# A decode step of attention plus a gated MLP on one core: loads of four heads instead of two, K transposed as 32-bit words, and the rest of the kernel fitted to that

## The chip, the core and the metric

The kernel runs on one core of one Trainium2 chip. The time is the device time of one execution in microseconds (us); the kernel before took 699.09 us (median of 3 runs, 698.64 to 700.31). A core has five engines with a queue of instructions each: TensorE (PE in the profile; its loading of the stationary operand is listed apart as PEld), VectorE (DVE), ScalarE (ACT), GpSimd (POOL) and SyncE (SP). Here SP issues nearly all DMAs. Engines wait for one another and for DMAs through semaphores only, and each takes its instructions in order.

## The reference

One token for each of 4 sequences. Attention reads a cache of 4,096 keys and values for each of 4 x 32 heads, 128 numbers each, in bf16: 128 MiB of K and 128 MiB of V. The second branch is a small gated MLP ("gMLP") on the same input.

```python
x = A_x                                  # 4 x 1 x 640
xn = layernorm(x)
q = (xn @ wq)  -> (4, 32 heads, 1, 128)
scores = q . k_cache * 128 ** -0.5       # k_cache 4 x 32 x 4096 x 128
p = softmax(scores)
o = p . v_cache                          # v_cache 4 x 32 x 4096 x 128
attention = o.reshape(4, 1, 4096) @ wo   # wo 4096 x 640
z = gelu(xn @ w_in)                      # w_in 640 x 1728
z1, z2 = z[..., :864], layernorm(z[..., 864:])
gmlp = (z1 * (w_sp * z2 + b_sp)) @ w_out # w_out 864 x 640
out = x + attention + gmlp
```

## The kernel before

**Units.** A unit is one 2 MB load of K or of V: two heads of one sequence, 128 partitions with 64 keys each, so that a partition's row is 16 KB (`load_unit`, L248, on SP's queue). There are 64 units of K and 64 of V. Eight units (four heads, four sequences) make a group; softmax is done once for each of the 8 groups, and V of a group runs `VDU` = 10 units behind its K. K has a pool of four 2 MB tiles, V another of four.

**K.** Scores need the head dimension on the partitions, so TensorE transposes K: a 128x128 block of bf16 is loaded as stationary operand, and the identity is streamed through it (L273, 64 blocks a unit, 8 to a PSUM tile `pst`, of which there are three). DVE and ACT take turns to copy the `pst` tiles to SBUF (`evacuate`, L262 and L264; tile `kT`). Then come the scores (`emit_S`, L293): the query, placed in a row of zeros (`qz_all`) so that each unit writes rows of its own, against `kT`, 512 columns at a time, four column groups side by side.

**Softmax** (`chain_stage`): a maximum over S, turned by TensorE (L308, a transpose of 128x1 fp32) and spread again by TensorE (L319), the exponential on ACT (L326), P transposed by TensorE (L337, 16 matmuls a group), and copied into `Zb`, in which zeros surround it, by DVE and ACT.

**V** (`emit_V`, L365): stationary is a 32-column window of `Zb`, moving is V, 512 columns at a time. After four units the result is copied (`emit_O`, L374, L375), its diagonal blocks are picked by fp32 matmuls (`emit_sel`, L383), divided by the row sums (L387) and multiplied with `wo` into `proj` (L396). At the end `proj` is cast (L447) and stored (L448, L449). The last unit of V comes in two loads.

**Start.** x and wq are loaded (L87, L94), the input is normalised, q is computed (L155). The weights of the gMLP are loaded at unit 2 into three tiles of V's pool (L174, L178), which wq still holds; the branch is computed at units 5 and 6 (L191, L201, L230), w_in being read with a stride of 9 columns.

**Order.** The program is written as one loop over half units, with a table `sched` of what is called at which half unit. SP takes its loads in that order, and a load whose tile isn't free holds up all behind it.

Of the kernel before, what the change touches and what calls it, by code (L numbers as in the profile page):

```python
# [8 lines left out]
ACT = mybir.ActivationFunctionType  # L9
# [7 lines left out]
def kernel(  # L17
# [13 lines left out]
):  # L31
    nc = tc.nc
# [3 lines left out]
    assert Sq == 1 and Dh == P and D % P == 0 and B == 4  # L36
    DC = D // P
    HP = 2
    M = P // HP
    T = Sk // M  # L40
    NP = 8
    TP = T // NP
    assert TP == 8
    HG = 4
    G = HG * B
    NG = H // HG
    NHP = HG // HP
    UPG = NHP * B
    NU = NG * UPG
    BLK = T // 4  # L50
    F2 = B_w_in.shape[1]
    Fh = F2 // 2
    FP = 96
    FC = Fh // FP
    assert FP * FC == Fh
# [5 lines left out]
    VDU = UPG + 2  # L61
# [6 lines left out]
    ppool = ctx.enter_context(tc.tile_pool(name="ppool", bufs=2))  # L68
    opool = ctx.enter_context(tc.tile_pool(name="opool", bufs=2))
    wopool = ctx.enter_context(tc.tile_pool(name="wopool", bufs=2))  # L70
# [11 lines left out]


# [5 lines left out]
    wq_v = A_wq.rearrange("(c p) n -> p c n", p=P)  # L89
    wq_t = []  # L90
    for i, (c0, c1) in enumerate(((0, 2), (2, 4), (4, 5))):
        wt = vpool.tile([P, 2, H * Dh], BF16, tag="v", name=f"wq{i}")
        for c in range(c0, c1):
            nc.sync.dma_start(out=wt[:, c - c0, :], in_=wq_v[:, c, :])  # L94
            wq_t.append(wt[:, c - c0, :])
# [10 lines left out]
    QS = 32  # L106
    qz_all = const.tile([P, (H * B + 1) * QS], BF16)
    nc.gpsimd.memset(qz_all[:], 0.0)
    ZB = T * 8 + 8
    Zb = []  # L110
    for i in range(2):
        zt = const.tile([P, NHP, B * ZB], BF16, name=f"Zb{i}")
        nc.gpsimd.memset(zt[:], 0.0)
        Zb.append(zt)
# [4 lines left out]
    I16 = const.tile([P, G], F32)  # L119
    nc.vector.tensor_tensor(out=I16[:], in0=I32[:, 0:16], in1=I32[:, 16:32], op=ALU.add)  # L120


    xf = const.tile([B, D], F32)
    nc.vector.tensor_copy(out=xf[:], in_=x_bf[:])  # L124
    ssum = small.tile([B, 1], F32, tag="ln_s")
    nc.vector.reduce_sum(out=ssum[:], in_=xf[:], axis=AX.X)
# [13 lines left out]
    for c in range(DC):  # L140
        nc.tensor.transpose(xT_ps[:, c, :], xn_bf[:, c * P:(c + 1) * P], ident_bf[:B, :B])  # L141
# [338 lines left out]
```

## Time and profile before

| | |
|---|---|
| median of 3 runs | 699.09 us (698.64 to 700.31) |
| the profiled execution | 698.35 us |
| its span, first to last instruction | 696.6 us |
| read from HBM | 282.24 MB, 405 GB/s over the span |
| busy: PE, PEld, DVE, ACT, POOL | 75%, 56%, 32%, 40%, 2% |
| loads of 2 MB from issue to landing, median | K 34.2 us, V 35.1 us |
| transposes of K (L273) | 4096, the wait before them mostly for the load of K |
| copies of `pst` to `kT` | 256 on ACT, 256 on DVE |

Read it as follows. The share of busy time says little by itself, since PE's spans overlap. The rows "GB/s" and "DMA" cut the span into 40 slices of 17.4 us: they show where the loads ran and where they didn't. The view of windows gives the same numbers for any stretch, with the TensorE clock that was granted in it (1.00 is full speed). The timeline gives single instructions, or runs of like ones, with start and duration.

### The profile page before, as it was taken

The numbers are of one execution on the slowest core, as the hardware profiler recorded it, in microseconds if no ns is written. First come the engines' busy times: TensorE is split into PE (matmuls) and PEld (weight loads), VectorE is DVE, ScalarE is ACT, GpSimd is POOL, SyncE is SP. The second block draws the span as 40 slices with busy tenths as digits, with TensorE's granted clock in tenths as the row PEclk, the third lists the DMA queues.
The fourth block names the chain that finished last, engine by engine and source line by source line (L and its number), as shares of the span: only waits on it lengthen the run. The fifth ranks groups of instructions, "written<-read, shape, count | busy, mean of one in ns | idle before, by whom it ended". The sixth has DMA issues, their size and how long they took to land.

```text
span 696.6 us, 15065 instructions
## 1 busy us (share of the span) xinstructions
PE 523.3 (75%) x6781; PEld 391.6 (56%) x6781; DVE 225.9 (32%) x384; ACT 278.3 (40%) x311; POOL 12.7 (2%) x13
## 2 busy tenths in 40 slices
PE   0998999877777776777778687778768787886644
PEld 0886777655655554556466466556556665664322
DVE  8312454333222432333323332224223332332100
ACT  0433676444343443444444354345334344443000
POOL 7000000000000000000000000000000000000000
PEclk9976999999899999998989998899988999899555
DMA  8996999999999999999999999999999999999992
GB/s 338 403 357 254 360 428 425 427 426 419 425 426 427 423 422 425 426 428 422 424 426 426 428 419 428 426 427 421 423 423 431 423 425 422 430 424 423 413 424 115
DMA packets 24456, 283.22 MB, mean 407 GB/s; under 512 B 2396, under 2 KB 6504, under 8 KB 7144
## 3 DMA queue, kind: packets, MB, share of 16 engines
q1 hardware_dynamic: 24320, 282.26, 96.9%
q8 instruction: 53, 0.87, 0.5%
q14 instruction: 11, 0.09, 0.0%
q0 software_dynamic: 64, 0.00, 0.0%
q10 hardware_dynamic: 8, 0.00, 0.0%
HBM read 282.24 MB, written 0.01 MB: 405 GB/s over the span
## 4 chain that ended last, share of the span: by engine, by line
DMA 77%; PE 18%; ACT 3%; issue 1%; DVE 1%; SPq 0%; ACTq 0%; DVEq 0%
DMA v<-in_A_v_cache_dram 42%; DMA k<-in_A_k_cache_dram 34%; PE pst L273 10%; ACT kT L262 3%; PE S L293 3%; PE misc L191 2%; PE O L365 2%; PE proj L230 0%; SPq L94 0%; PE misc L383 0%; DVE Zb L264 0%; PE ptp L337 0%; ACT Zb L262 0%; PE proj L396 0%; PE misc L201 0%
## 5 line engine op out<-in xcount | busy, mean ns | idle before, releaser
L262 ACT COPY kT<-pst 128x1024 bf16<-128x1024 bf16 x256 | 254.4, 1012 | 305.0 <-PE pst L273 304.6
L273 PE MATMUL pst<-ident_bf,k 128*128 128x128 bf16 x4096 | 300.8, 239 | 95.9 <-DMA k<-in_A_k_cache_dram 90.8
L273 PEld LDWEIGHTS <-k 128*128 128x128 bf16 x4096 | 275.4, 109 | 141.0 <-DMA k<-in_A_k_cache_dram 111.1
L264 DVE COPY kT<-pst 128x1024 bf16<-128x1024 bf16 x256 | 177.1, 692 | 330.7 <-PE pst L273 330.5
L293 PE MATMUL S<-kT,qz_all 128*32 128x512 bf16 x1024 | 110.7, 385 | 8.1 <-ACT kT L262 8.1
L365 PE MATMUL O<-v,Zb 128*32 128x512 bf16 x1024 | 80.0, 418 | 19.1 <-DMA v<-in_A_v_cache_dram 19.1
L365 PEld LDWEIGHTS <-Zb 128*32 128x32 bf16 x1024 | 31.8, 101 | 52.0 <-issue 28.8
L293 PEld LDWEIGHTS <-qz_all 128*32 128x32 bf16 x1024 | 32.7, 95 | 37.8 <-issue 17.8
L383 PEld LDWEIGHTS misc<-I,O_sb 128*128 128x128 f32 x128 | 18.5, 216 | 13.9 <-ACT O_sb L374 12.5
L374 ACT COPY O_sb<-O 128x256 f32<-128x256 f32 x16 | 6.0, 373 | 45.9 <-PE O L365 45.8
L375 DVE COPY O_sb<-O 128x256 f32<-128x256 f32 x16 | 6.8, 424 | 51.6 <-ACT O_sb L374 50.9
L383 PE MATMUL misc<-I,O_sb 128*128 128x8 f32 x128 | 20.5, 280 | 3.3 <-ACT O_sb L374 2.9
L191 PEld LDWEIGHTS <-w_in 128*96 128x96 bf16 x90 | 15.6, 267 | 0.8 <-DMA w_in<-in_B_w_in_dram 0.4
L191 PE MATMUL misc<-xnT,w_in 128*96 128x4 bf16 x90 | 15.8, 312 | 0.0
L326 ACT ACTIVATE p_bf<-S,negmax 128x512 bf16<-128x512 f32 x8 | 5.5, 687 | 21.6 <-DVE negmax L322 21.6
L141 PE MATMUL misc<-ident_bf,xn_bf 4*128 4x4 bf16 x5 | 0.3, 165 | 14.6 <-DVE xn_bf L138 14.6
L264 DVE COPY Zb<-ptp 64x256 bf16<-64x256 bf16 x16 | 6.7, 417 | 13.7 <-PE ptp L337 10.6
L396 PE MATMUL proj<-wo,oT 128*4 128x320 bf16 x64 | 7.8, 326 | 4.1 <-DVE oT L387 4.1
L124 DVE CAST xf<-x_bf 4x640 f32<-4x640 bf16 x1 | 10.3, 10287 | 1.2 <-DMA x_bf<-in_A_x_dram 1.2
L337 PE MATMUL ptp<-ident_bf,p_bf 128*64 128x128 bf16 x128 | 9.6, 225 | 1.1 <-ACT p_bf L326 1.1
L348 PE MATMUL misc<-ds,ones_f 128*128 128x16 f32 x16 | 4.0, 329 | 8.0 <-DVE ds L329 8.0
L337 PEld LDWEIGHTS <-p_bf 128*64 128x64 bf16 x128 | 7.3, 111 | 4.5 <-issue 2.8
(70 smaller groups left out, 79.8 us busy)
## 6 DMA issues: line engine op xcount, KB each, us to landing
k<-in_A_k_cache_dram SPq DMA_DIRECT2D x64, 2048.0 KB, 34.2
v<-in_A_v_cache_dram SPq DMA_DIRECT2D x63, 2048.0 KB, 35.1
wq<-in_A_wq_dram SPq DMA_DIRECT2D x5, 1024.0 KB, 11.1
wo<-in_A_wo_dram SPq DMA_DIRECT2D x8, 640.0 KB, 36.0
v<-in_A_v_cache_dram SPq DMA_DIRECT2D x2, 1024.0 KB, 17.3
w_in<-in_B_w_in_dram SPq DMA_DIRECT2D x1, 1296.0 KB, 31.1
w_out<-in_B_w_out_dram SPq DMA_DIRECT2D x1, 1080.0 KB
w_in<-in_B_w_in_dram SPq DMA_DIRECT2D x1, 864.0 KB
```

The costliest lines, as they stand in the source:

```text
L124: nc.vector.tensor_copy(out=xf[:], in_=x_bf[:])
L191: nc.tensor.matmul(zT_ps[:FP, part * FC + fc, :], lhsT=w[:, fc, :], rhs=xnT[:, c, :], start=(c == 0), stop=(c == DC - 1))
L262: nc.scalar.copy(out=dst, in_=src)
L264: nc.vector.tensor_copy(out=dst, in_=src)
L273: nc.tensor.transpose(pst[:, e, :], k_sb[:, pc * TP + e, :], ident_bf[:])
L293: nc.tensor.matmul(S_ps[32 * q:32 * q + 32, :, :], lhsT=qz_all[:, w0:w0 + 32], rhs=kT[:, :, hd, :], start=(ul == 0 and bt == 0 and hd == 0 ...
L337: nc.tensor.transpose(ptp[hd * M:(hd + 1) * M, e, :], p_bf[:, e, :], ident_bf[:])
L365: nc.tensor.matmul(O_ps[32 * q:32 * q + 32, :, :], lhsT=Z[:, hp, w0:w0 + 32], rhs=vv[:, half, e, :, :], start=(b == 0 and half == 0 and e ...
L374: nc.scalar.copy(out=O_sb[:, 0:2, :], in_=O_ps[:, 0:2, :])
L375: nc.vector.tensor_copy(out=O_sb[:, 2:4, :], in_=O_ps[:, 2:4, :])
L383: nc.tensor.matmul(oh[:], lhsT=O_sb[:, j, :], rhs=sel[:, j, :, :], start=(j == 0), stop=(j == 3))
L396: nc.tensor.matmul(proj[32 * hf:32 * hf + B, 0:NO2], lhsT=oT[:, hd, :], rhs=wo_t[:, hp * HP + hd, hf * NO2:(hf + 1) * NO2], start=False, s ...
```

## The change

- **Loads.** A unit is now four heads of one sequence: 4 MB, 128 keys on a partition, rows of 32 KB (L278). There are 32 units of K, 32 of V, four to a group. K, V, wq and the gMLP's weights share one pool of five 4 MB tiles. wq comes in two loads with rows of 24 and 16 KB; its rows are dealt to partitions in another order, and so are xn's columns.
- **K as words.** The K tile is read as fp32: one word is two neighbouring bf16 numbers of a key. A 128x128 block of words is transposed with the fp32 identity (L303); 64 blocks a unit of twice the size, four to a `pst` tile of 2 KB a partition. `pst` is copied as 1024 bf16 as before (L292, L294). In `kT` the even and the odd numbers of a key alternate, and a partition holds one word. So the query is permuted by a matmul (L182), and the scores take two matmuls that read every second number of `kT` (L321). Two zero-padded tiles `QZ` are filled for each group by POOL (L191).
- **P.** The maximum goes through 32x32 transposes on DVE (L329, L336) instead of TensorE, and P is turned by one DVE transpose of 128x512 (L349). POOL copies it into `Zb`, four copies for each pair of sequences (L362).
- **V.** As before (L386), with a whole 512-column matmul over four keys' rows. The last unit differs: V itself is stationary, 128 blocks of 128x128, and four columns of P are streamed (L479). It comes in loads of 64, 32, 16 and 16 keys. The result needs neither the copy nor the picking.
- **gMLP.** Its weights are loaded behind unit 7 of K, and it runs in the middle of the stream. w_in is loaded as rows of 17,280 bytes and read without stride.

What SP issues at the start, before (the names are the tiles with their numbers; L94 is wq, L174 and L178 are the gMLP's weights):

```order
L94 DMA wq_96<-in_A_wq_dram 128x4096 x2
L94 DMA wq_99<-in_A_wq_dram 128x4096 x2
L94 DMA wq_102<-in_A_wq_dram 128x4096
L248 DMA k_325<-in_A_k_cache_dram 128x8192
L248 DMA k_424<-in_A_k_cache_dram 128x8192
L248 DMA k_530<-in_A_k_cache_dram 128x8192
L174 DMA w_in_576<-in_B_w_in_dram 128x3x1728
L174 DMA w_in_578<-in_B_w_in_dram 128x2x1728
L178 DMA w_out<-in_B_w_out_dram 96x5760
L248 DMA k_644<-in_A_k_cache_dram 128x8192
L248 DMA k_750<-in_A_k_cache_dram 128x8192
```

And now, from wq to the second load of V:

```order
L97 DMA wq_93<-in_A_wq_dram 128x12288
L97 DMA wq_95<-in_A_wq_dram 128x8192
L278 DMA k_335<-in_A_k_cache_dram 128x16384
L278 DMA k_464<-in_A_k_cache_dram 128x16384
L278 DMA k_598<-in_A_k_cache_dram 128x16384
L278 DMA k_732<-in_A_k_cache_dram 128x16384
L278 DMA k_868<-in_A_k_cache_dram 128x16384
L278 DMA v_959<-in_A_v_cache_dram 128x16384
L278 DMA k_1049<-in_A_k_cache_dram 128x16384
L278 DMA v_1137<-in_A_v_cache_dram 128x16384
```

No load of gMLP weights stands between the first loads of K any more. Further on in the same queue, around the eighth and ninth unit of K, they stand now:

```order
L278 DMA v_1309<-in_A_v_cache_dram 128x16384
L278 DMA k_1400<-in_A_k_cache_dram 128x16384
L208 DMA w_gmlp<-in_B_w_in_dram 128x8640
L211 DMA w_gmlp<-in_B_w_out_dram 128x6x640
L212 DMA w_gmlp<-in_B_w_out_dram 96x640
L278 DMA v_1490<-in_A_v_cache_dram 128x16384
L278 DMA k_1574<-in_A_k_cache_dram 128x16384
```

They take one of the five tiles, between a load of K and one of V.

The last instructions of PE before, from the last matmul with V on:

```order
L365 LDWEIGHTS Zb_122
L365 MATMUL O<-v_8972,Zb_122 32x512
L383 MATMUL misc_8994<-I_124,O_sb 128x8 x4
L396 LDWEIGHTS oT
L396 MATMUL proj<-wo_8764,oT 4x320
```

And now: picking (L465) and eight matmuls for the three earlier sequences, then 128 pairs for the last unit of V, then eight matmuls (the pairs and the projections are shown once each):

```order
L465 MATMUL misc_6281<-I_136,O_sb 128x8 x4
L411 LDWEIGHTS oT
L411 MATMUL proj<-wo_6197,oT 4x320
...
L479 LDWEIGHTS v_6274
L479 MATMUL ol<-Zb_154,v_6274 128x4
...
L411 LDWEIGHTS oL
L411 MATMUL proj<-wo_6197,oL 4x320
```

Picking has moved ahead of the last unit's matmuls; behind them stand one DVE multiplication (L480) and the eight matmuls of the projection.

The core of the diff:

```diff
-    HP = 2
-    M = P // HP
+    HG = 4
+    M = P // HG
     T = Sk // M
-    kpool = ctx.enter_context(tc.tile_pool(name="kpool", bufs=4))
-    vpool = ctx.enter_context(tc.tile_pool(name="vpool", bufs=4))
-    ktpool = ctx.enter_context(tc.tile_pool(name="ktpool", bufs=10))
+    kvpool = ctx.enter_context(tc.tile_pool(name="kvpool", bufs=5))
+    ktpool = ctx.enter_context(tc.tile_pool(name="ktpool", bufs=2))
...
+    def load_gmlp_weights():
+        wt = kv_tile("w_gmlp")
+        n_in = DC * F2
+        w_in = wt[:, 0:n_in].rearrange("p (c f) -> p c f", c=DC)
+        nc.sync.dma_start(out=w_in, in_=B_w_in.rearrange("(p c) f -> p c f", c=DC))
+        w_out = wt[:, n_in:n_in + FC * NOUT].rearrange("p (c n) -> p c n", c=FC)
+        nf = (FC - 1) * P
+        nc.sync.dma_start(out=w_out[:, 0:FC - 1, :], in_=B_w_out[0:nf, :].rearrange("(c p) n -> p c n", p=P))
+        nc.sync.dma_start(out=w_out[:FL, FC - 1, :], in_=B_w_out[nf:Fh, :])
...
+    def load_unit(cache, key, u, cuts=(0, T)):
+        g, b = divmod(u, B)
+        t_sb = kv_tile(f"{key}{u}")
+        src = cache[b, g * HG:(g + 1) * HG].rearrange("e (m t) d -> (e m) (t d)", t=T)
+        for t0, t1 in zip(cuts[:-1], cuts[1:]):
+            nc.sync.dma_start(out=t_sb[:, t0 * Dh:t1 * Dh], in_=src[:, t0 * Dh:t1 * Dh])
...
+    def emit_T(u, ch):
+        kw = state[("k", u)][:].bitcast(F32)
+        kT = ktpool.tile([P, KP, HG, M, 2], BF16, tag="kT", name="kT")
+        for pc in range(4):
+            pst = ps_t.tile([P, 4, P], F32, tag="pst", name="pst")
+            for e in range(4):
+                k = ch * KP + pc * 4 + e
+                nc.tensor.transpose(pst[:, e, :], kw[:, k * P:(k + 1) * P], ident_f[:])
+            evacuate(kT[:, pc * 4:(pc + 1) * 4].rearrange("p e h m w -> p (e h m w)"),
+                     pst[:].rearrange("p e m -> p (e m)").bitcast(BF16))
...
+        for w in range(2):
+            for hd in range(HG):
+                w0 = 16 + (hd * B + b) * 32 - (b * NCH + ch)
+                nc.tensor.matmul(S_ps[32 * hd:32 * hd + 32, :, :], lhsT=qz[:, w, w0:w0 + 32],
+                                 rhs=kT[:, :, hd, :, w], start=(b == 0 and ch == 0 and w == 0),
+                                 stop=(b == B - 1 and ch == NCH - 1 and w == 1))
...
+        nc.vector.transpose(x[:].rearrange("p e b c -> p (e b c)"), p_bf[:].rearrange("p k m -> p (k m)"))
...
+    def z_fill(g, bb):
+        x = state[("x", g)]
+        for hd in range(HG):
+            r0 = 32 * hd
+            dst = Zb[bb][r0:r0 + 32, :].rearrange("p (b y) -> p b y", y=ZL)[:, :, 0:1024].rearrange(
+                "p b (e c) -> p e b c", c=32)[:, :, :, hd * 4:hd * 4 + 4]
+            nc.gpsimd.tensor_copy(out=dst, in_=x[r0:r0 + 32, :, 2 * bb:2 * bb + 2, :])
...
-    at(2 * 2, load_gmlp_weights)
-    at(2 * 5, gmlp_branch)
-    at(2 * 6, gmlp_out)
+    at(NCH * 7, load_gmlp_weights)
+    at(NCH * 8 + 2, gmlp_branch)
+    at(NCH * 8 + 3, gmlp_out)
...
+    TAIL = (0, 64, 96, 112, 128)
...
+            for t in range(T):
+                c, e = divmod(t, 32)
+                zc = Zb[1][:, ZL + e * 32:ZL + e * 32 + 16].rearrange("p (h c) -> p h c", c=NCH)[:, :, c]
+                nc.tensor.matmul(ol_ps[:], lhsT=vv[:, t, :], rhs=zc, start=(t == 0), stop=(t == T - 1))
+            nc.vector.tensor_tensor(out=oL[:, :, 3:4], in0=ol_ps[:, :, None], in1=rinv[:, :, 3:4], op=ALU.mult)
+            emit_proj(g, oL, last=True)
```

More of the change, by code (lines that the diff above doesn't have):

```diff
@@ L81, in misc_ps, with kv_tile @@
         return ps_m.tile(shape, dtype, tag="misc", name=f"misc{misc_ctr[0]}")
+    KV = T * Dh
+    def kv_tile(name):
+        return kvpool.tile([P, KV], BF16, tag="kv", name=name)
     x_flat = A_x.rearrange("b s d -> (b s) d")
@@ L353, in emit_V @@
-    def emit_V(v, half):
-        g, hp, b, h = unit_info(v)
-        if b == 0 and half == 0:
+        kT = state.pop(("kT", u, ch))
+        qz = QZ[g % 2]
+        for w in range(2):
+            for hd in range(HG):
[3 more added lines that the diff above has]
+                                 stop=(b == B - 1 and ch == NCH - 1 and w == 1))
```

456 lines of the change are left out of this document (216 added, 240 removed).

## The prediction

> **What bounds the kernel now.** I read the page's slices first, then the chain that ended last, then the windows.
>
> ```profile
> PEclk9976999999899999998989998899988999899555
> DMA  8996999999999999999999999999999999999992
> GB/s 338 403 357 254 360 428 425 427 426 419 425 426 427 423 422 425 426 428 422 424 426 426 428 419 428 426 427 421 423 423 431 423 425 422 430 424 423 413 424 115
> DMA v<-in_A_v_cache_dram 42%; DMA k<-in_A_k_cache_dram 34%; PE pst L273 10%; ACT kT L262 3%; PE S L293 3%; PE misc L191 2%; PE O L365 2%; PE proj L230 0%; SPq L94 0%; PE misc L383 0%; DVE Zb L264 0%; PE ptp L337 0%; ACT Zb L262 0%; PE proj L396 0%; PE misc L201 0%
> ```
>
> From the sixth slice to the last but one the loads run at 413 to 431 GB/s with all DMA engines busy, and three quarters of the chain are loads of K and V. This is a kernel bound by its loads, except in the first five slices and the last. What the change can win lies there; what it can lose is the rate in between. The windows price the two ends:
>
> ```profile
> 15.00:20.00 5.00, 2.52 (x89) 2.53 (x90) 2.42 (x10) 0.29 (x1) 0.00 (x0) 1.00 0.79 320
> 30.00:52.00 22.00, 21.60 (x223) 18.66 (x220) 5.54 (x8) 9.16 (x9) 0.00 (x0) 0.82 1.01 363
> 52.00:60.00 8.00, 5.42 (x30) 5.16 (x30) 1.60 (x10) 1.81 (x3) 0.00 (x0) 0.50 1.02 430
> 60.00:68.00 8.00, 7.62 (x91) 5.60 (x92) 2.99 (x6) 2.95 (x4) 0.00 (x0) 0.72 0.27 113
> 68.00:90.00 22.00, 20.40 (x295) 15.22 (x288) 9.76 (x15) 14.14 (x15) 0.00 (x0) 1.00 0.95 354
> 100.00:640.00 540.00, 416.35 (x5543) 314.88 (x5544) 176.89 (x298) 234.03 (x261) 0.00 (x0) 0.91 1.01 425
> 676.00:690.00 14.00, 6.12 (x52) 1.72 (x47) 0.00 (x0) 0.00 (x0) 0.00 (x0) 0.50 0.57 238
> ```
>
> The last three columns are granted clock, DMA share and GB/s. Against 425, 60 to 68 us loses 8 x (1 - 113/425) = 5.9 us, 68 to 90 loses 22 x (1 - 354/425) = 3.7, 30 to 52 loses 3.2 though the engines were busy there (short rows), 15 to 20 loses 1.2. The timelines of SP and PE name the cause of the big hole:
>
> ```profile
> 6.19 16.32 SPq L174 DMA_DIRECT2D w_in<-in_B_w_in_dram  x2
> 22.62 0.40 SPq L178 DMA_DIRECT2D w_out<-in_B_w_out_dram  x1
> 23.07 57.02 SPq L248 DMA_DIRECT2D k<-in_A_k_cache_dram  x7
> ...
> 17.77 4.41 PE L155 MATMUL misc<-xnT,wq 128*128 128x4 bf16 x160 [0.26 <-DVE xnT L143]
> ...
> 41.62 15.12 PE L191 MATMUL misc<-xnT,w_in 128*96 128x4 bf16 x87
> ...
> 60.38 2.56 PE L230 MATMUL proj<-w_out,uT 96*4 96x320 bf16 x18 [2.25 <-DVE uT L223]
> ```
>
> w_in waits for wq's tiles until q is done, with K loads behind it. Then PE spends 41.6 to 62.9 us on the gMLP, transposes nothing, and K's four tiles stay full.
>
> **The change part by part.** The sum starts from the profiled execution's own 698.35 us (span 696.6 and 1.75 around it), 0.74 below the median of the runs.
>
> *Start and gMLP.* Ahead of the first wait SP now issues wq and three units of K, 17.8 MB; at 425 GB/s they last until about 45 us. The fourth K waits for wq's tile, so for q, done at 22.2 us; if PE is two units late, that still hides. The gMLP's weights follow unit 7 of K; their tile is the next but four to be used again, so 39 us of loads (four of 4.19 MB / 425 GB/s = 9.87 us) cover its use. Its 70 matmuls read without stride; at q's 4.41 us / 160 they take 2 us, and even at L191's pace 12; chain and second part add some 5. While PE waits in them, V and the next K are in flight. So 5.9 + 3.7 go. Of the 3.2 I take 2.5: w_in gets long rows, w_out does not (bounds 0 and 3.2). The 1.2 stay: POOL's two tiny loads of w_sp and b_sp are issued behind its memsets as before. Together **12.1 us**.
>
> *K on PE.* This is the price the trace doesn't show: an fp32 transpose of 128x128 in a row of such. The nearest rows:
>
> ```profile
> L308 PE MATMUL misc<-ident_f,m x8: 270/270/272, 95.2 to 641.8; 128*1 128x128 f32 x8
> ...
> L273 PE MATMUL pst<-ident_bf,k x4096: 216/219/314, 22.7 to 639.0; 128*128 128x128 bf16 x196
> ...
> 128.89 1.07 PE L273 MATMUL pst<-ident_bf,k 128*128 128x128 bf16 x16
> 129.88 0.62 PE L293 MATMUL S<-kT,qz_all 128*32 128x512 bf16 x8
> 130.33 1.04 PE L365 MATMUL O<-v,Zb 128*32 128x512 bf16 x16
> ...
> 131.85 1.07 PE L383 MATMUL misc<-I,O_sb 128*128 128x8 f32 x8
> ...
> 690.61 1.88 PE L383 MATMUL misc<-I,O_sb 128*128 128x8 f32 x8 [0.47 <-ACT O_sb L374]
> ```
>
> A single fp32 transpose with 128 streamed columns takes 270 ns against 219 for bf16: streaming costs some 50 ns more, about 105 in a row where bf16 takes (1.07 - 0.22) / 15 = 0.057. Loading 128 fp32 columns as stationary is shown by L383: (1.07 - 0.26) / 7 = 0.116 us a pair at full clock, (1.88 - 0.38) / 7 = 0.214 at half clock. If loading and streaming overlap, as in the bf16 rows, a transpose takes **0.116**; bounds are 0.057 and, one after the other at half clock, about 0.42. I take 0.116, the nearest row. Then a unit of K needs 64 x 0.116 = 7.4 us, where 64 blocks of half the bytes took 3.7. The scores keep their number of matmuls for each byte: 32 in eight rounds of four, (0.62 - 0.38) = 0.24 a round at most, 1.9 us; V the same, (1.04 - 0.38) / 3 = 0.22 a round, 1.8. PE needs 11.1 us for a unit of K and one of V, whose loads take 19.7. While only K is loaded (four and a half units), it needs 9.3 of 9.9. Copies from `pst` are as many and as large for each byte: eight on ACT at 1.012 us and eight on DVE at 0.692 a unit, inside the 9.9:
>
> ```profile
> L262 ACT COPY kT<-pst 128x1024 bf16<-128x1024 bf16 x256 | 254.4, 1012 | 305.0 <-PE pst L273 304.6
> ...
> L264 DVE COPY kT<-pst 128x1024 bf16<-128x1024 bf16 x256 | 177.1, 692 | 330.7 <-PE pst L273 330.5
> ```
>
> So this part costs **nothing on the path**, and its cover is 8 us in 19.7. Reading every second number of `kT` is not shown; doubled scores would be 1.9 more, still covered. If PE fell behind in the K phase, five tiles hold 39 us of loads; even 16 us a unit would stall the loads by 3 to 5 us only.
>
> *Softmax.* Removed: 16 transposes of P and two small PE steps a group; added: three DVE transposes and eight POOL copies of 256 numbers a partition. The large DVE transpose lies between nothing and the 0.692 of a copy of 1024; a POOL copy I put under 1 us. On PE a whole unit of K (9 us) stands between the last scores and the first use of `Zb`, and covers them. POOL has nothing else to do. A single `wo` tile makes SP wait for the last projection, with K behind it; that projection comes right behind the last V of its group, with two loads (19 us) still in flight.
>
> *Rate.* Rows of 8 KB (wq) and of 16 KB moved:
>
> ```profile
> 4.00:15.00 11.00, 0.00 (x0) 0.00 (x0) 10.83 (x6) 0.00 (x0) 9.29 (x5) 1.00 1.01 425
> 110.00:150.00 40.00, 35.03 (x505) 25.79 (x508) 14.69 (x23) 20.74 (x23) 0.00 (x0) 0.96 1.01 426
> ```
>
> One more doubling may bring half of that 0.2% again, **0.8 us** (bounds 3 us either way). Instructions are fetched by DMA too:
>
> ```profile
> q8 instruction: 53, 0.87, 0.5%
> ```
>
> From 676 to 690 us only 57% of the DMA engines still work: some end about 14 x 0.43 = 6 us behind the others. If fetching makes them late, 4590 matmuls in the program instead of 6700 take 31% of it away, **1.9 us** (bounds 0 and 1.9).
>
> *The end.* From the landing of the last V:
>
> ```profile
> 689.09 1.05 PE L365 MATMUL O<-v,Zb 128*32 128x512 bf16 x8 [1.43 <-DMA v<-in_A_v_cache_dram]
> ...
> 690.59 0.42 DVE L375 COPY O_sb<-O 128x256 f32<-128x256 f32 x1 [16.68 <-ACT O_sb L374]
> ...
> 692.74 0.70 PE L396 MATMUL proj<-wo,oT 128*4 128x320 bf16 x4 [0.26 <-DVE oT L387]
> 693.48 0.48 DVE L447 CAST o_bf<-proj 64x320 bf16<-64x320 f32 x1 [0.80 <-PE proj L396]
> ```
>
> Before: 693.48 - 689.09 = 4.4 us to the cast, 3.1 behind it. Now the last 16 pairs take 0.44 (q's 28 ns each), draining and the multiplication 0.5, eight projections instead of four 0.70 + 0.5: 2.2 us. The rest stays. **2.2 us** go (bounds 1.5 and 2.5).
>
> Sum: 698.35 - 12.1 - 0.8 - 1.9 - 2.2 = 681.35, forecast **681.3 us**, 2.4% less.
>
> **The rivals.**
>
> *PE at half clock becomes the bound (slower).* Half clock is granted where PE mostly loads weights: 52 to 60 us, in L191, at 0.50. An fp32 transpose spends more on loading than on streaming. At half clock a pair of units takes 64 x 0.214 = 13.7 plus 16 rounds of scores and V at 0.42 (eight matmuls of L365 in 1.05 us above, two rounds at clock 0.5) = 6.7 plus 0.3 for the rest, 20.7 us against 19.7 for its loads: 1.0 x 27.5 pairs = 27 us, **708 us**. It turns slower once a pair passes 19.7 + 17 / 27.5 = 20.3 us, so only if the clock stays low almost throughout; at full clock a transpose would have to take (20.3 - 4.0) / 64 = 0.25 us. Against it: 68 to 90 us, full of transposes, had clock 1.00, and a PE that is the bound is never idle. The Trainium skill ("TensorE: Matmul & The Clock Gate", Part 4: PE-mode transpose) says that transposes do not count as PE being busy, so the full clock does not engage; by that rule this rival would be the forecast. The row of 68 to 90 us speaks against the rule.
>
> *Loading and streaming do not overlap.* Then a transpose takes 0.116 + 0.105 = 0.22 us, a pair 18.1 at full clock: covered, but the K phase needs 16 us a unit, and any low clock shows. 3 to 12 us more: **684 to 693 us**. Nothing in the trace shows two fp32 transposes in a row, so nothing decides.
>
> *The hole only moves.* Five tiles for K, V and gMLP together may be held longer than I think around unit 8, or in the K phase. Half of the 9.6 us idle comes back: **686 us**. For it: SP takes loads strictly in order. Against: the reckoning of 39 us.
>
> **How the numbers follow.** Forecast (loads bound throughout) 0.73; the hole moves 0.06; no overlap 0.09; half clock or a price above 0.25 us 0.10; a loss of rate with the long rows that ends within 0.3% of before or above, 0.02. The forecast's own range: 681.3 with the 0.7 of w_out and 3 of the rate below and 6 us of uneven ending gone gives 673; with 3 of the rate, 2.5 and 1.9 unearned 689. The middle rivals reach to 693, so the range is 673 to 693. A difference under 0.3% (2.1 us) can't be told from none. Faster 0.87, same 0.02, slower 0.11.
>
> **What would show it.** Right: 420 GB/s or more in every slice from the second to the last but one, no hole around 60 us nor at the gMLP's new place; L303 in runs at about 0.12 us each; PE waiting for loads of K in the middle; some 5.3 us from the last landing to the end. Wrong: SP waiting for transposes while the DMA share is under 0.9; L303 at 0.2 us or more; clock 0.5 through the middle; slices below 410 GB/s with the engines busy, which would put it on the 32 KB rows.

## The result and the profile after

The changed kernel takes **677.74 us** (median of four runs, 677.69 to 678.79) against 698.87 (697.99 to 700.31) for the kernel before in the same session: ratio 0.970, 95% interval 0.968 to 0.972. The profiled execution took 678.79 us with a span of 676.9.

The page of the kernel after, its slices, the queue of instruction fetches and the shares of the chain that ended last:

```profile
PEclk9999998788878989688898878987787998967865
DMA  8999999999999999999999999999999999999994
GB/s 324 431 429 429 433 423 429 407 430 432 416 429 431 431 433 417 429 434 431 429 419 433 427 431 428 422 433 432 429 417 431 431 429 433 423 425 432 409 417 171
...
q8 instruction: 36, 0.59, 0.4%
...
DMA 58%; PE 32%; ACT 6%; DVE 3%; issue 1%; SPq 0%; ACTq 0%; DVEq 0%
```

No slice from the second to the last but one is below 407 GB/s, and the hole of before (357, 254 and 360 GB/s in the third to the fifth slice) is gone. The prediction had asked for 420 or more in each; seven lie between 407 and 419. PE's share of the chain has grown from 18% to 32% while DMA is still busy throughout: PE is later than before, but the loads do not wait for it.

Windows price it. Three that follow each other and cover the span before, then five after; the last three columns are the granted clock, the share of the DMA engines and GB/s:

```profile
0.00:90.00 90.00, 67.45 (x877) 55.88 (x878) 38.62 (x61) 33.68 (x36) 12.72 (x13) 0.89 0.89 346
90.00:660.00 570.00, 437.72 (x5776) 327.73 (x5777) 185.59 (x318) 243.92 (x274) 0.00 (x0) 0.90 1.01 425
660.00:696.60 36.60, 18.09 (x136) 8.00 (x128) 1.66 (x5) 0.74 (x2) 0.00 (x0) 0.50 0.65 275
```

```profile
0.00:90.00 90.00, 61.72 (x659) 45.45 (x663) 39.10 (x81) 43.78 (x45) 8.27 (x26) 1.00 0.97 410
90.00:120.00 30.00, 26.56 (x256) 19.10 (x244) 11.51 (x18) 15.90 (x16) 0.00 (x0) 0.94 1.01 425
120.00:160.00 40.00, 27.67 (x287) 19.54 (x281) 10.67 (x30) 15.25 (x19) 3.79 (x10) 0.79 1.01 417
160.00:640.00 480.00, 363.99 (x3214) 259.81 (x3212) 155.37 (x265) 199.45 (x211) 20.73 (x55) 0.86 1.01 429
640.00:676.90 36.90, 21.56 (x264) 12.10 (x264) 1.72 (x6) 0.58 (x1) 0.74 (x2) 0.55 0.71 293
```

A stretch of t us at r GB/s loses t x (1 - r/425) against the old steady rate. That gives a ledger of the two profiled executions, which lie 698.35 - 678.79 = 19.6 us apart:

| | before, us lost | after | gain | predicted |
|---|---|---|---|---|
| start (0 to 90 us) | 16.7 | 3.2 | 13.5 | |
| gMLP at its new place (120 to 160) | | 0.8 | -0.8 | |
| start and gMLP together | | | **12.7** | 12.1 |
| rate in the middle (160 to 640) | | -4.5 | **4.5** | 0.8 |
| the last 37 us | 12.9 | 11.5 | 1.4 | |
| 283.22 MB - 282.92 MB, fewer instruction fetches | | | 0.7 | |
| end and fetches together | | | **2.1** | 1.9 + 2.2 |

The gains add up to 19.3 us. The rates are rounded to 1 GB/s, which in the row of the middle leaves about 0.6 us open. The profiled execution of the kernel after is the slowest of its four, 1.05 us above their median; the ledger does not cover that part.

### The profile page after: what moved, and what is told of

Its sections match the earlier page's. It is cut to its first block, busy times and chain, and to the rows that moved or that the text cites. A ratio compares the mean times of both kernels' runs of the same rounds, so it can differ in the third digit from the quotient of the medians.

```text
span 676.9 us, 10603 instructions
## 1 busy us (share of the span) xinstructions
PE 501.5 (74%) x4663; PEld 356.0 (53%) x4663; DVE 218.4 (32%) x398; ACT 275.0 (41%) x291; POOL 33.5 (5%) x92
## 2 busy tenths in 40 slices
DMA packets 15333, 282.92 MB, mean 418 GB/s; under 512 B 1356, under 2 KB 6328, under 8 KB 6584
## 4 chain that ended last, share of the span: by engine, by line
DMA 58%; PE 32%; ACT 6%; DVE 3%; issue 1%; SPq 0%; ACTq 0%; DVEq 0%
DMA k<-in_A_k_cache_dram 55%; PE pst L303 19%; PE S L321 5%; ACT kT L292 4%; PE O L386 3%; DMA v<-in_A_v_cache_dram 3%; PE misc L403 1%; PE proj L411 1%; DVE kT L294 1%; ACT p_bf L341 1%; PE ol L479 1%; DVE m L327 1%; DVE x L349 0%; PE misc L368 0%; PE misc L227 0%
## 5 line engine op out<-in xcount | busy, mean ns | idle before, releaser
L292 ACT COPY kT<-pst 128x1024 bf16<-128x1024 bf16 x256 | 254.9, 1013 | 325.9 <-PE pst L303 243.3
L303 PE MATMUL pst<-ident_f,k 128*128 128x128 f32 x2048 | 313.1, 310 | 99.9 <-DMA k<-in_A_k_cache_dram 95.2
L303 PEld LDWEIGHTS pst<-ident_f,k 128*128 128x128 f32 x2048 | 265.9, 160 | 164.0 <-issue 122.2
L294 DVE COPY kT<-pst 128x1024 bf16<-128x1024 bf16 x256 | 176.9, 692 | 334.9 <-PE pst L303 321.1
L321 PE MATMUL S<-kT,QZ 128*32 128x512 bf16 x1024 | 95.2, 385 | 13.0 <-ACT kT L292 9.9
L386 PE MATMUL O<-v,Zb 128*32 128x512 bf16 x992 | 67.4, 411 | 10.1 <-DMA v<-in_A_v_cache_dram 10.1
L386 PEld LDWEIGHTS <-Zb 128*32 128x32 bf16 x992 | 31.0, 101 | 39.0 <-issue 15.3
L321 PEld LDWEIGHTS <-QZ 128*32 128x32 bf16 x1024 | 20.9, 94 | 49.8 <-issue 38.0
L362 POOL COPY Zb<-x 32x256 bf16<-32x256 bf16 x64 | 25.2, 394 | 184.0 <-DVE ds L351 153.5
L191 POOL COPY QZ<-q 64x32 bf16<-64x32 bf16 x16 | 5.1, 320 | 422.6 <-PE S L321 402.4
L294 DVE COPY O_sb<-O 128x512 f32<-128x512 f32 x8 | 5.5, 692 | 36.8 <-PE O L386 36.8
L341 ACT ACTIVATE p_bf<-S,negmax 128x512 bf16<-128x512 f32 x8 | 5.5, 687 | 15.9 <-DVE negmax L338 15.8
L368 PEld LDWEIGHTS misc<-ds,ones_f 128*128 128x128 f32 x16 | 2.9, 225 | 16.8 <-DVE ds L351 16.3
L176 PE MATMUL misc<-xnT,wq 128*128 128x4 bf16 x160 | 4.6, 166 | 8.2 <-DMA wq<-in_A_wq_dram 4.5
L349 DVE STREAM_TRANSPOSE x<-p_bf 128x512 bf16<-128x512 bf16 x8 | 5.7, 712 | 9.7 <-ACT p_bf L341 9.7
```

What stands on the lines that cost most here:

```text
L176: nc.tensor.matmul(q_ps[:, h, :], lhsT=wq_t[c][:, h * Dh:(h + 1) * Dh], rhs=xnT[:, c, :], start=(c == 0), stop=(c == DC - 1))
L292: nc.scalar.copy(out=dst, in_=src)
L294: nc.vector.tensor_copy(out=dst, in_=src)
L303: nc.tensor.transpose(pst[:, e, :], kw[:, k * P:(k + 1) * P], ident_f[:])
L321: nc.tensor.matmul(S_ps[32 * hd:32 * hd + 32, :, :], lhsT=qz[:, w, w0:w0 + 32], rhs=kT[:, :, hd, :, w], start=(b == 0 and ch == 0 and w == 0),
L341: nc.scalar.activation(out=p_bf[:].rearrange("p k m -> p (k m)"), in_=S_ps[:].rearrange("p k m -> p (k m)"), func=ACT.Exp, bias=negmax[:, ...
```

## The experiments

Every time is a median; a ratio is to the kernel before, run in the same session. The yardstick is the changed kernel once more:

> The changed kernel once more, as the yardstick of this series: 677.7 us, ratio 0.970.

It took 678.65 us (678.58 to 678.71), ratio 0.9712 (0.9699 to 0.9725). With the 677.74 above, the changed kernel stands at 677.7 to 678.7, and one microsecond between two variants of different sessions means little.

### Rows of 16 KB instead of 32 KB

```diff
-            load_unit(A_k_cache, "k", u)
+            load_unit(A_k_cache, "k", u, cuts=(0, T // 2, T))
```

and the same for V.

> Every 4 MB load of K and V is issued as two loads of half a row, so rows of 16 KB as before the change; nothing else differs. If the better rate in the middle (428 against 425 GB/s) comes from the row length, it falls back to about 425 and the time rises by 664 x 0.007 = 4 to 5 us, to 682. If it comes from something else (fewer fetches of instructions, fewer waits), the time stays at 678 within 1 us.

It took 683.9 us, ratio 0.9785 (0.9772 to 0.9798): 5.2 us more than the yardstick. The window of its middle:

```profile
100.00:640.00 540.00, 411.96 (x3612) 282.13 (x3606) 171.81 (x303) 220.36 (x234) 23.80 (x62) 0.87 1.01 424
```

424 GB/s, the old rate, with everything else as changed. The single packets, one for each row, show where it comes from. Between 160 and 640 us a packet of 16 KB takes 617 ns on average in the kernel before and in this variant; one of 32 KB takes 1,221 ns in the kernel after, 13 ns less than two of 16 KB. Each of the 16 engines moves 504 of the large ones, so that is an estimated 6.6 us. The rate in the middle is won by the length of the rows, not by the larger tiles or the shared ring. (Each load is half as large here too; no run parts that from the rows.)

### The last wo later

```diff
-        at(NCH * B * g + VD + 4, lambda g=g: load_wo(g))
+        at(NCH * B * g + VD + 9, lambda g=g: load_wo(g))
```

> The load of wo stands five quarter units later in SP's queue, behind one more load of V. In the changed kernel SP waited 77 us in all for the last projection before it could issue wo, and the loads dipped to about 300 GB/s at 641 to 643 us. If that wait lets the loads run dry, the dip goes and 1.5 to 2 us with it (676). If the wait is covered by the loads in flight, nothing changes (677.7).

677.74 us, ratio 0.9698 (0.9685 to 0.9712), 0.9 us less than the yardstick. The dip at 641 to 643 us (287 GB/s in the kernel after) is not here (459), but the yardstick's own profile has none either (401), so the dip is not what cost the 0.9 us. The last landing stayed near 670 us. What differs is the last but one load of V: TensorE starts on it at 659.22 us, against 661.06 in the kernel after and 660.86 in the yardstick. It is through with all earlier work sooner and then waits for the last pieces, as its timeline shows:

```profile
665.78 1.87 PE L479 MATMUL ol<-Zb,v 128*128 128x4 bf16 x64 [0.58 <-DMA v<-in_A_v_cache_dram]
668.28 1.01 PE L479 MATMUL ol<-Zb,v 128*128 128x4 bf16 x32 [0.63 <-DMA v<-in_A_v_cache_dram]
669.54 0.59 PE L479 MATMUL ol<-Zb,v 128*128 128x4 bf16 x16 [0.25 <-DMA v<-in_A_v_cache_dram]
670.81 0.59 PE L479 MATMUL ol<-Zb,v 128*128 128x4 bf16 x16 [0.67 <-DMA v<-in_A_v_cache_dram]
```

The last pair ends at 671.40 us; in the kernel after it ends at 672.27.

### The two tiny loads of POOL

```diff
-    nc.gpsimd.dma_start(out=wsp_bf[:], in_=B_w_sp.rearrange("a b -> (a b)").to_broadcast((P, 1)))
-    nc.gpsimd.dma_start(out=bsp_bf[:], in_=B_b_sp.to_broadcast((P, 1)))
     def load_gmlp_weights():
+        nc.sync.dma_start(out=wsp_bf[:], in_=B_w_sp.rearrange("a b -> (a b)").to_broadcast((P, 1)))
+        nc.sync.dma_start(out=bsp_bf[:], in_=B_b_sp.to_broadcast((P, 1)))
```

> The two tiny loads of w_sp and b_sp are issued by SP with the gMLP's other weights instead of by POOL at the start. If they cause the dip of the loads at 7 to 10 us (263, 30 and 294 GB/s, while their 16-byte packets were moving), the dip goes and 1.6 us with it (676). If the dip belongs to the first loads themselves, it stays (677.7).

677.42 us, ratio 0.9694 (0.9681 to 0.9708), 1.2 us less than the yardstick. The same window of the kernel after and of this one:

```profile
3.00:15.00 12.00, 0.60 (x8) 0.43 (x8) 6.51 (x26) 0.29 (x1) 0.83 (x2) 1.00 0.82 345
```

```profile
3.00:15.00 12.00, 0.59 (x8) 0.43 (x8) 6.16 (x24) 0.29 (x1) 0.00 (x0) 1.00 0.98 418
```

While two loads of 0.2 KB are under way on POOL's queue, the others are held up: (1 - 345/425) x 12 = 2.3 us are lost, against 0.2 us in the same window without them. On SP's queue they are issued at 90 us and landed by 127 us; from 95 to 160 us the loads run at 421 GB/s, against 423 in the kernel after, some 0.3 us. Queue and time changed together, so no run says which of the two matters. The 1.2 us lost before at 15 to 20 us, which the prediction left in place, fall on the time of the same two loads in the kernel before; the change moved these loads forward, to 7 to 12 us.

### The end as before

The last V unit as two loads and 512-column matmuls like any other:

```diff
-        if 0 <= v < NU - 1:
+        if 0 <= v < NU:
...
-        elif v == NU - 1 and vc == 0:
...
+            load_unit(A_v_cache, "v", v, cuts=(0, T // 2, T) if v == NU - 1 else (0, T))
```

> The changed kernel with the old end: the last V unit comes as two loads of 16 KB rows and is multiplied by 512-column matmuls with P stationary, then copied, picked and projected as every other unit; everything else as changed. The prediction had the new end worth 2.2 us: then this takes 678.7 + 2.2 = about 680.9 us. The trace of the changed kernel says that after the last landing (about 670.3) TensorE still owes the picking and eight projection matmuls of the half before, so that the new end saves only what lies between 6.5 us and the old one's time behind its last landing: then +0.5 to +1.5 us, 679.2 to 680.2. If the end is set by the DMA engines that come late alone, 678.7 within 0.3.

682.17 us, ratio 0.9765 (0.9753 to 0.9778): 3.5 us more than the yardstick, and more than any of the three cases gave it. Its timeline and, below it, that of the kernel after:

```profile
670.83 3.60 PE L386 MATMUL O<-v,Zb 128*32 128x512 bf16 x32 [6.21 <-DMA v<-in_A_v_cache_dram]
675.17 1.06 PE L403 MATMUL misc<-I,O_sb 128*128 128x8 f32 x8 [0.74 <-ACT O_sb L292]
676.49 0.71 PE L411 MATMUL proj<-wo,oT 128*4 128x320 bf16 x8 [0.26 <-DVE oT L404]
```

```profile
661.06 3.60 PE L386 MATMUL O<-v,Zb 128*32 128x512 bf16 x32 [5.32 <-DMA v<-in_A_v_cache_dram]
665.41 1.87 PE L465 MATMUL misc<-I,O_sb 128*128 128x8 f32 x8 [0.74 <-ACT O_sb L462]
667.54 1.23 PE L411 MATMUL proj<-wo,oT 128*4 128x320 bf16 x8 [0.26 <-DVE oT L468]
668.70 3.57 PE L479 MATMUL ol<-Zb,v 128*128 128x4 bf16 x128
672.53 1.23 PE L411 MATMUL proj<-wo,oL 128*4 128x320 bf16 x8 [0.26 <-DVE oL L480]
```

The whole last unit is released at once, 32 matmuls at half clock, 3.60 us, where the kernel before had eight left, 1.05 us. Twofold of that comes with the 4 MB unit. The other twofold lies in the order of the keys, as the code has it: in `emit_V` each matmul takes keys from all four quarters of a row, so none can start before both loads have landed, where before the second load held up only its own half. The new end avoids that cost; against the kernel before it saves little: 696.6 - 689.1 = 7.5 us from the last landing to the end of the span there, about 676.9 - 670.3 = 6.6 in the kernel after. In the kernel after, nothing in the last three rows waits for a load (the row of L479 names no releaser): TensorE is still busy with the unit before, and runs behind the last landing.

### The kernel before with the gMLP late

```diff
-    at(2 * 2, load_gmlp_weights)
-    at(2 * 5, gmlp_branch)
-    at(2 * 6, gmlp_out)
+    at(2 * 14, load_gmlp_weights)
+    at(2 * 17, gmlp_branch)
+    at(2 * 18, gmlp_out)
```

> The kernel before with one thing of the change alone: the gMLP weights are loaded ahead of K unit 14, and the branch and its output follow at units 17 and 18, in place of units 2, 5 and 6. Theory: the slices at 60 to 90 us lost 9.6 us because the gMLP chain held up the buffers of the loads at a time when nothing else was loaded far ahead; moved, the same chain meets a full ring of loads and most of it is hidden: 698.8 - 9.6 = about 689 us (687 to 691), with slices of 420 GB/s or more at 60 to 90 us. Rival: the hole comes from the shape of the gMLP loads or from its buffer, and moves along with them: 698.8 within 1.5, and a hole of some 10 us at the new place (about 200 to 260 us).

700.82 us, ratio 1.0028 (1.0017 to 1.004): nothing won, 0.3% lost. The hole came along: the old place loses next to nothing now, also at 30 to 52 us (425 GB/s). Its windows and the two rows of SP and PE that make it:

```profile
60.00:68.00 8.00, 7.60 (x113) 5.90 (x111) 4.15 (x6) 5.03 (x6) 0.00 (x0) 1.00 1.01 409
68.00:90.00 22.00, 21.07 (x313) 16.12 (x316) 12.00 (x22) 17.33 (x20) 0.00 (x0) 1.00 1.01 426
...
120.00:160.00 40.00, 21.89 (x187) 19.26 (x186) 3.95 (x7) 5.59 (x6) 0.00 (x0) 0.67 0.92 320
160.00:200.00 40.00, 36.55 (x478) 28.53 (x479) 15.13 (x35) 20.64 (x25) 0.00 (x0) 0.90 0.90 368
```

```profile
147.00 0.43 SPq L248 DMA_DIRECT2D k<-in_A_k_cache_dram  x1
163.59 0.33 SPq L248 DMA_DIRECT2D v<-in_A_v_cache_dram  x1
```

```profile
148.43 15.47 PE L191 MATMUL misc<-xnT,w_in 128*96 128x4 bf16 x90 [0.37 <-DVE mx L310]
```

Loss at the new place: 40 x (1 - 320/425) + 40 x (1 - 368/425) = 15.3 us. From 147.4 to 163.6 us SP issues nothing: the next V tile is one of those that hold the weights, and L191 reads them until about then.

### The changed kernel with the gMLP early

```diff
-    at(NCH * 7, load_gmlp_weights)
-    at(NCH * 8 + 2, gmlp_branch)
-    at(NCH * 8 + 3, gmlp_out)
+    at(NCH, load_gmlp_weights)
+    at(NCH * 2 + 2, gmlp_branch)
+    at(NCH * 2 + 3, gmlp_out)
```

> The changed kernel with the gMLP put back near the start: its weights are loaded behind K unit 0 and its branch comes at K unit 2 (of 16), its output one step later, in place of units 7 and 8. It tells where from how: the new form of the branch (weights in a buffer of the ring, 128-row pieces) stays, only the place goes back. Theory that the place alone made the hole: a hole of 5 to 10 us comes back in the slices at 40 to 100 us, 684 to 689 us. Rival, that the form of the load and the short chain (about 9 us of branch against a ring of five units of 9.8 us) cure it anywhere: 678.7 within 1.5 us.

678.41 us, ratio 0.9707 (0.9694 to 0.9719): the same as the yardstick. Its slices show one dip for the weights (403 in the third slice, where the kernel after has 407 in its eighth), and no hole:

```profile
GB/s 327 433 403 429 432 430 420 432 435 431 411 434 432 430 432 418 432 433 430 430 417 431 432 430 422 432 430 429 430 421 432 432 428 430 426 427 430 416 417 185
```

So "midway" is worth nothing by itself, in either kernel.

### The kernel before with neighbouring columns

```diff
-                    w = gw[("in", c)][:, part * Fh:(part + 1) * Fh].rearrange("p (k r) -> p r k", r=FC)
-                    nc.tensor.matmul(zT_ps[:FP, part * FC + fc, :], lhsT=w[:, fc, :],
+                    f0 = part * Fh + fc * FP
+                    nc.tensor.matmul(zT_ps[:FP, part * FC + fc, :], lhsT=gw[("in", c)][:, f0:f0 + FP],
...
-        nc.sync.dma_start(out=wt[:], in_=B_w_out.rearrange("(p c) n -> p c n", c=FC))
+        nc.sync.dma_start(out=wt[:], in_=B_w_out.rearrange("(c p) n -> p c n", c=FC))
```

> The kernel before with the gMLP's hidden units split into nine runs of 96 neighbouring columns instead of every ninth column (and w_out's rows taken to match, so they come as 1280-byte rows instead of 11520-byte rows); place, tiles and order as before. Theory: TensorE's 15.1 us for 87 matmuls with strided stationary columns is what empties the loads at 60 to 90 us (K's four tiles stay full meanwhile); with neighbouring columns they take some 2 to 3 us, the 5.9 + 3.7 us of the two windows go, and of the 3 us that w_out's rows lose at 36 to 44 us two come back: 698.7 - 9.6 - 2 = 687 us (685 to 690). Rival: the hole comes from the three V tiles that the weights occupy and from SP's strict order, whatever the matmuls take: 697 to 698.7 us with the hole still there.

690.93 us, ratio 0.9887 (0.9873 to 0.99): this edit alone wins 7.9 us, 0.9 us less than the least that was expected. Timeline and windows:

```profile
40.76 5.86 PE L191 MATMUL misc<-xnT,w_in 128*96 128x4 bf16 x87
```

```profile
30.00:52.00 22.00, 18.46 (x252) 14.43 (x251) 6.74 (x18) 10.70 (x12) 0.00 (x0) 0.78 1.03 344
...
60.00:68.00 8.00, 7.60 (x117) 6.02 (x112) 3.74 (x6) 4.58 (x5) 0.00 (x0) 1.00 1.01 425
68.00:90.00 22.00, 20.75 (x296) 15.17 (x294) 11.31 (x19) 15.65 (x17) 0.00 (x0) 1.00 1.01 420
```

The 87 matmuls take 5.86 instead of 15.12 us, and of the 9.6 us lost at 60 to 90 us 0.3 are left. But 30 to 52 us got worse, 4.2 instead of 3.2 us: the expectation that w_out's rows would move faster missed. The clock is not what made the old columns slow: their shortest load of a stationary operand takes 246 ns, the longest here 196, at half clock.

### The changed kernel with strided columns

The reverse: in the changed kernel the gMLP gets the old pieces back (nine of every ninth column, w_out on 96 partitions), in its one tile of the ring.

```diff
-    FC = (Fh + P - 1) // P
+    FP = 96
+    FC = Fh // FP
...
-                    nc.tensor.matmul(zT_ps[:n, part, fc, :], lhsT=gw["in"][:, c, f0:f0 + n],
+                    w = gw["in"][:, c, part * Fh:(part + 1) * Fh].rearrange("p (k r) -> p r k", r=FC)
+                    nc.tensor.matmul(zT_ps[:FP, part, fc, :], lhsT=w[:, fc, :],
...
+        nc.sync.dma_start(out=w_out[:FP], in_=B_w_out.rearrange("(p c) n -> p c n", c=FC))
```

> The changed kernel, gMLP midway and its weights in one tile of the ring as changed, but its hidden units split as before: nine pieces of every ninth column, w_out as 11520-byte rows. TensorE then spends 15 us instead of 2.3 in these matmuls. Theory that five tiles of 4 MB (39 us of loads behind the one in use) cover a stop of TensorE of that length: no hole there, only w_out's rows lose some 3 instead of 1.2 us: 678.2 + 2 = about 680 us (679 to 681.5). Rival, that the hole follows the strided columns wherever they stand (in the kernel before with the gMLP late it came along): a hole of 5 us or more after 140 us, 683 us or more.

681.91 us, ratio 0.9763 (0.9746 to 0.978), 3.3 us more than the yardstick and 0.4 above the range that was given. Timeline, then windows:

```profile
140.85 6.53 PE L224 MATMUL misc<-xnT,w_gmlp 128*96 128x4 bf16 x37
147.30 1.05 PE L317 MATMUL S<-kT,QZ 128*32 128x512 bf16 x8
148.28 9.28 PE L224 MATMUL misc<-xnT,w_gmlp 128*96 128x4 bf16 x53
```

```profile
130.00:142.00 12.00, 12.00 (x88) 8.98 (x86) 5.53 (x8) 8.41 (x9) 0.00 (x0) 0.89 1.03 265
142.00:180.00 38.00, 32.88 (x229) 26.18 (x229) 8.90 (x27) 10.14 (x13) 3.79 (x10) 0.64 1.00 431
```

TensorE is held for 15.8 us, and the loads run on at 431 GB/s: the ring covers a stop that emptied the old pools. What is lost lies ahead of the matmuls, in the loading of w_out, with every engine busy (share 1.03): 12 x (1 - 265/429) = 4.6 us.

### K's transposes half as many again, and twice

```diff
-                nc.tensor.transpose(pst[:, e, :], kw[:, k * P:(k + 1) * P], ident_f[:])
+                for rep in range(1 + e % 2):
+                    nc.tensor.transpose(pst[:, e, :], kw[:, k * P:(k + 1) * P], ident_f[:])
```

and `range(2)` for the second.

> The changed kernel with every second fp32 transpose of K done twice, so that a K unit has 96 in place of 64: at 0.125 us each that is 4.0 us more of TensorE for each K unit, where K and V together have 19.6 us of loads. The prediction had about 8 us of cover there: then nothing is to be seen beyond the longer instruction stream (about 8 more packets of instruction fetch, some 1.3 us): 678.7 to 680.7 us. Rival, that TensorE is already near the bound (busy to 9.3 of 9.9 us while only K is worked on, or the clock falls as it works more): 16 x 4.0 = up to 64 us more where it has no cover, and at least 4 x 3.5 = 14 us from the units of the first group alone: 692 us or more.

> The changed kernel with every fp32 transpose of K done twice (128 for a K unit in place of 64). At 0.125 us each a K unit takes 16 us on TensorE for its transposes, 20 us with the scores and V of its partner, against 19.6 us of loads: the cover that the prediction counted (8 us) is spent to the last. Theory: 3 to 5 us more in each of the four or five units at the start where K stands alone, partly held by the ring (5 to 15 us), and 0 to 1 us for each of the 27 pairs: 690 to 715 us. If it stays under 682 us, TensorE had more cover than reckoned (the clock rises as it works more: 0.92 with half as many again); if it is above 720 us the transposes cost more than the 0.125 us that a run shows.

With 96 a unit: 679.45 us, ratio 0.9729 (0.9717 to 0.9742), 0.8 us more than the yardstick. With 128: **715.86 us**, ratio 1.0249 (1.0226 to 1.0271), 37 us more and slower than the kernel before, 0.9 us above the range that was given. The middle of the first; then of the second the timeline, the shares of the chain, two windows and the slices:

```profile
100.00:640.00 540.00, 465.22 (x4582) 363.04 (x4574) 176.17 (x308) 235.21 (x245) 22.09 (x58) 0.93 1.00 427
```

```profile
37.59 3.71 PE L304 MATMUL pst<-ident_f,k 128*128 128x128 f32 x32
```

```profile
PE 87%; DMA 6%; ACT 3%; DVE 3%; issue 1%; SPq 0%; DVEq 0%; ACTq 0%
```

```profile
30.00:90.00 60.00, 60.00 (x565) 52.28 (x564) 20.07 (x29) 28.41 (x29) 0.00 (x0) 1.00 1.01 432
100.00:640.00 540.00, 512.63 (x5212) 425.01 (x5212) 169.55 (x298) 226.60 (x236) 25.90 (x68) 0.97 0.96 408
...
GB/s 331 432 433 427 429 398 253 388 415 429 422 430 429 429 432 134 416 433 418 434 421 434 431 423 427 429 427 429 432 423 429 425 432 429 379 432 411 221 258 251
```

Doubled, a transpose costs (3.71 - 0.27) / 31 = 0.111 us, and the chain is TensorE to 87%. Half as many again is nearly free. But the cover is not spent everywhere: from 300 to 600 us of the doubled variant the loads still run at 428 GB/s, with TensorE busy 282 of 300 us. The 408 GB/s come from a few slices of 17.9 us. The sixth to the eighth (398, 253, 388, from 89 to 143 us) lie around the end, at 109 us, of the stretch in which only K is worked on: there the ring has run out. In the sixteenth (134) SP issues nothing from 258.3 to 284.8 us: it waits for the last projection (L412) before it can load `wo` into its single tile, with K behind it. It waits in the same way from 658.2 to 684.5 us, over the whole of the thirty-eighth (221). So a part of the 37 us is the price of the single `wo` tile, with a TensorE that comes late to the projection; no run separates it.

### The edits together

wo later, the tiny loads on SP, and at the end O of the half before copied as bf16, picked by bf16 matmuls, and projected together with the last batch:

```diff
-            O_sb = opool.tile([P, 4, Dh], F32, tag="O_sb", name="O_sb", bufs=2)
+            O_sb = opool.tile([P, 4, Dh], BF16, tag="O_sb", name="O_sb", bufs=2)
...
-            emit_proj(g, oT)
...
-            emit_proj(g, oL, last=True)
+            emit_proj(g, oT, last=True)
```

> The changed kernel with four edits: wo is loaded five steps later; w_sp and b_sp are loaded by SP beside the gMLP weights; at the end O of the half before is copied as bf16 and picked by bf16 matmuls (four at the cost of a bf16 one instead of eight at 0.23 us), and its projection is joined with that of the last batch (eight matmuls of L411 less ahead of the last pairs). The first two gave 0.9 and 1.2 us by themselves. The last two let the 128 pairs of L479 begin at about 665.9 instead of 668.7, so that they wait for the last landing (670.3) and end at about 671 instead of 672.3: 1.3 us. Together 678.2 - 3.4 = about 675 us (674 to 676.5). If the last landing is what counts in all of them, the gains don't add: 676.5 to 677.5.

677.04 us, ratio 0.9688 (0.9675 to 0.9701): 1.6 us less than the yardstick, and not to be told apart from the single edits: the gains do not add, as the second case of the expectation had it. Its end:

```profile
669.71 0.59 PE L477 MATMUL ol<-Zb,v 128*128 128x4 bf16 x16 [0.67 <-DMA v<-in_A_v_cache_dram]
670.55 1.23 PE L413 MATMUL proj<-wo,oT 128*4 128x320 bf16 x8 [0.26 <-DVE oT L478]
```

With wo later alone the last 16 pairs waited for their load already (670.81 above), so a faster end on TensorE has nothing left to win: what counts is when the last DMA engine lands.

## Why the prediction held, point by point

**Bound by loads: right.** TensorE waits for K in the middle of the kernel after, and the loads run on.

**Start and gMLP, 12.1 forecast, 12.7 in the ledger: right in size and in the main mechanism.** The prediction put the hole on TensorE being held from 41.6 to 62.9 us while K's tiles stay full, and gave two covers: matmuls without stride, and five tiles with 39 us of loads. Each is shown alone: neighbouring columns in the old kernel win 7.9 us, and the ring carries a stop of 15.8 us without a hole. Moving the gMLP, alone, wins nothing in either kernel. The small term was right for a wrong reason: the 3.2 us at 30 to 52 us were put on "short rows". Rows of 3456 bytes were hardly slow: their packets took 143 ns on average in the kernel before, 24 bytes a ns, where K's and V's took 617 ns for 16 KB, 27 bytes a ns. w_out was slow: its packets of 11520 bytes took 767 ns, 15 bytes a ns. While it was loaded all loads together fell, with 11520-byte rows (265 GB/s in the strided variant, window 130 to 142) and with 1280-byte rows alike (344 GB/s over 30 to 52 us against 363). Both put it on 96 partitions; in the changed kernel most of it goes to 128, and the whole window of 120 to 160 us loses 0.8. That the 96 partitions are the cause fits all four traces; it was not tried by itself.

**K on TensorE: right; less cover than reckoned while only K is worked on, about as much in the middle.** The price that no trace of before showed, 0.116 us for an fp32 transpose, is 0.111 to 0.133. K phase and middle of the kernel after:

```profile
41.78 4.39 PE L303 MATMUL pst<-ident_f,k 128*128 128x128 f32 x32
46.10 0.62 PE L321 MATMUL S<-kT,QZ 128*32 128x512 bf16 x8
46.65 2.15 PE L303 MATMUL pst<-ident_f,k 128*128 128x128 f32 x16
...
53.08 4.40 PE L303 MATMUL pst<-ident_f,k 128*128 128x128 f32 x32
```

```profile
217.82 5.20 PE L303 MATMUL pst<-ident_f,k 128*128 128x128 f32 x28 [4.87 <-DMA k<-in_A_k_cache_dram]
```

A run of 16 takes 2.15 us, (2.15 - 0.27) / 15 = 0.125 each: loading and streaming overlap, and the rival at 0.22 falls. But a unit alone takes 53.08 - 41.78 = 11.3 us, not 9.3, so TensorE falls 1.5 us behind in each unit of the K phase, and the ring, not spare time, covers it. The prediction held the copies of `pst` to be hidden because they fit into 9.9 us; they are not wholly hidden. In the doubled variant a unit takes 54.35 - 37.59 = 16.8 us; without the 64 transposes more, at 0.111, that is an estimated 9.7. The other 1.6 us would be TensorE waiting for copies, of which its timeline shows 0.55 ahead of a unit's last scores.

In the middle TensorE is busy 363.99 / 480 = 76% of the time, 14.9 of 19.6 us a pair where 11.1 were reckoned. That is not work alone. In the doubled variant, 282 of 300 us are 18.4 of 19.6 us a pair, and without the 64 transposes more (7.1 us) an estimated 11.3 are left, as reckoned. What the 76% hold beyond that is in part the low clock after each wait: in the row above, 28 transposes take 5.20 us behind 4.87 us of idling, 0.18 each. The granted clock fell to 0.50 2.1 us after the last matmul ahead of that wait and came back to 1.00 4.0 us after work had begun. The Trainium skill ("TensorE: Matmul & The Clock Gate", Part 1: The HAM clock gate) says that the clock halves after some 3.4 us of idling and comes back after as much sustained work; the return agrees, the fall came sooner.

**Half clock as the bound: fell, by the argument given.** The prediction held that a TensorE that is the bound never idles, so its clock comes up. The more transposes, the higher the clock: 0.86, 0.93 and 0.97 in the middle for 64, 96 and 128 a unit, and 1.00 in the window of 30 to 90 us of the doubled variant, in which TensorE does nothing but transposes and scores (the scores take 0.5 of every 4.2 us). The rule of the Trainium skill in "TensorE: Matmul & The Clock Gate", Part 4: PE-mode transpose, that transposes do not engage the full clock, does not hold here.

**Rate, 0.8 forecast, 4.5 in the ledger and 5.2 when undone: this is the step that failed, in size.** The step from 8 KB to 16 KB (425 to 426 GB/s) was taken as the slope, from one window that stood at the start of the kernel. Doubling again was worth 1%, not 0.1%; it lies outside the bounds of 3 us that were given. The single packets would have shown it: in the kernel before the median is 309 ns for 8 KB and 613 for 16 KB, 0.8% less for each byte, and 1,216 for 32 KB in the kernel after is 0.8% less again. Two slices (407 and 409) fell under the 410 that was to speak against the rows of 32 KB, the first where the gMLP's weights are loaded; 429 over the middle says that the rows are not slow. The forecast is 3.6 us too high mainly for this. Of that, 2.6 lie between 681.35 and the profiled 678.79: 3.7 too little for the rate and 0.6 for start and gMLP, less the 2.0 too much in the next point, and 0.3 that the ledger leaves open. The other 1.05 us lie between the profiled execution and the median. That two errors of opposite sign partly cancel is luck.

**Fetches and end, 1.9 + 2.2 forecast, 2.1 in the ledger: about half.** The fetches fell from 53 to 36 packets, the unevenness with them: share 0.57 in 676 to 690 us before, 14 x 0.43 = 6.0 us, and 0.56 in 662 to 671 us after, 9 x 0.44 = 4.0. That the fetches are the cause is not shown, since no run changes them alone. The end saves little against the kernel before, because TensorE enters it late; 3.5 us are lost if it is undone. The prediction took the old end with the old 2 MB units as its base, and never priced what a 4 MB unit would do there; from the last landing to the end it had 5.3 us, and about 6.6 were measured.

## What to carry to other kernels

A hole in the loads is cured by what holds the buffers, not by where the work stands: ask how long the engine reads them and how many units of load lie in the ring, and test the two apart. Price a stationary operand with strided columns before anything else about it, since 87 small matmuls cost 15 us with stride and 6 without. A busy share is not a price: it holds waits and a low clock, and here it overstated TensorE's work for a pair by almost a third. Once loads bound a kernel to its end, shortening the chain behind the last landing pays only until the chain waits for that landing.

## What was not expected of the hardware

- With two broadcast loads of 0.2 KB on POOL's queue the loads of SP run at 345 GB/s over 12 us, 2.3 us lost; with these two on SP's own queue, and later, some 0.3.
- While a load onto 96 partitions is under way, all loads together move 265 GB/s over 12 us (rows of 11520 bytes) or 267 over 10 us (rows of 1280 bytes), with all 16 DMA engines busy. That the 96 partitions are the cause is not isolated.
- Rows of 32 KB run at 429 GB/s in the middle, rows of 16 KB at 424 to 425; a packet of 32 KB takes 1,221 ns, two of 16 KB take 1,234.
- TensorE's mean clock rises with its load: 0.86, 0.93, 0.97 with 64, 96 and 128 transposes a unit.
